# First LayerNorm fed feature first from the host, with its factor moved behind the matmuls, and a new order of loads and splits around the output projection of a pre-norm block

## The chip, the core and the metric

The kernel runs on one core of a Trainium2 chip, as one program in one launch. The metric is the device time of an execution in microseconds (us); lower is better. The kernel before was timed in three runs (median 1134.21 us, 1131.7 to 1136.86), and one more execution was profiled. TensorE (PE) does the matmuls, VectorE (DVE) and ScalarE (ACT) the elementwise work, GpSimd (POOL) a little of it, and SyncE (SP) issues all the DMAs shown here, in one queue: SP handles its instructions in order, and an instruction that has to wait holds up all behind it. The same is true of the other engines.

## The reference

One token sequence of 2048 tokens with 640 features passes through attention and a gated MLP, both behind a LayerNorm without parameters:

```python
def layernorm(x): return (x - mean(x)) / sqrt(var(x) + 1e-5)      # over the 640 features
qkv = layernorm(x) @ wqkv                    # 32 heads of 20 features
p   = softmax(where(0 <= i - j < 256, q @ k.T * 20**-0.5, -1e9))  # sliding window of 256
h   = x + (p @ v) @ wo
z   = gelu(layernorm(h) @ w_in)              # 1728 = 2 * 864 columns
g   = w_sp @ layernorm(z[:, 864:]) + b_sp    # 2048 x 2048 mixing of the tokens
out = h + (z[:, :864] * g) @ w_out
```

Everything is float32. The kernel keeps that accuracy with split products: an operand is written as a rounded part `hi` and a rest `lo`, and a product is hi\*hi + hi\*lo + lo\*hi, three matmuls.

## The kernel before

The 2048 tokens are 16 tiles of 128 (`NT`), the 640 features 5 blocks of 128 (`KD`). The order on PE, DVE, ACT and SP is the order in which the code is written (`manual_schedule`), so nothing overtakes anything on one engine; only POOL's order is left to a scheduler. The stages, with their place in the profiled execution:

- **V stage (0 to 92 us).** Per token tile i: `load_x` brings x token first (128 tokens x 640), `ln1` makes mean and variance (`bn_stats`, `bn_aggr`, + eps, and the power -1/2 on POOL, L74 to L77) and writes `xn = (x - mean) * rstd` in one DVE instruction (L80). `turn1` transposes the five blocks of xn on PE (L469, five matmuls with `ident`), and ACT and DVE take `hi` and `lo` out of PSUM into `xn_hi`, `xn_lo` (L473, L474), feature first. `vgemm` (L485 to L487) is two halves of 320 columns, 5 blocks, 3 products: 30 matmuls; ACT puts the result into `v_sb` (L488). The tiles 0 and 1 come while the weights `wv` are still being split (L560, L561). Also here: `wo` is loaded, split and stored to `wo_d` for later, and the first three pieces of `wqk` are loaded and split.
- **Q and K stage (92 to 245 us).** `qk_item(m, c)`: 128 of the 1280 q and k columns (m, 0 to 9) by 512 tokens (c, 0 to 3), 15 matmuls (L525 to L527). `split_qk` divides the result into three bf16 parts: ACT takes the first (L539), DVE the rest (L541), ACT the second (L543), POOL the third (L544); a DMA stores them in `qk_d`. From about 190 us on (`dense_tail`) each of the last twelve items is mixed, five steps an item, with `max_item`s of the attention: one score matmul and one DVE reduction each (L333, L339).
- **Attention (245 to 478 us).** 128 units s, each one block of 128 keys for four heads: row maxima, scores, exp on ACT, a mask on POOL, and p times v on PE (L425, `pv_item`), two units behind the scores. The last 15 units have no maxima left and wait for ACT. The sums of p come out as an extra row of v, row `DH` of `o_d`.
- **Output projection (473 to 562 us).** Per token tile: `norm_o` multiplies o by 1/sum (L162), `split_o` makes hi and lo (L168, L170, L171), `proj_o` is 30 matmuls (L100), `add_h` adds x (L1227) and stores h, `bn_h` and `scaled` make its LayerNorm, `turn_h` transposes it (L844) and stores it feature first in `hn_d`. In between lie the loads of o, of the sums (`rs`; for tokens from 512 on the reciprocals are formed once, `inv`, and go through `r_d`), of x again (`load_x2`), and `win1_prep`: w_in's first half, loaded in three steps into one buffer `wraw` (L780, L786) and turned into 16 tiles of split combinations (L715, L721, L136, L137). The first tiles' share of this runs inside the last attention units, as a generator `proj_early` that takes one step per unit from unit 97 on; the reciprocals of later tokens are further generators, `inverse_sums`.
- **MLP (562 to 1130 us).** `z_pair`, `z2_pair`, `first_gate`, `second_gate`: lists of steps that this change leaves as they are, but for three calls at the start of the list (`turn_h` of the last tile, and the opening of a pool).

## Time and profile before

| | |
|---|---|
| median of 3 runs | 1134.21 us (1131.7 to 1136.86) |
| the profiled execution | 1132.73 us; span 1130.9 us, so 1.8 us lie outside the span |
| granted TensorE clock, mean | 0.997 |
| PE busy | 1093.7 us, 97% of the span |
| DVE / ACT / POOL busy | 732.2 / 565.9 / 296.6 us |
| DMA | 171.78 MB |

In the rows that follow, a timeline row is: start in us, duration in us (of the whole group if it ends in xN), engine, line, operation, output<-input, shapes; in brackets how long the engine had been idle and who released it. Matmul durations overlap, so a matmul's cost is read from the starts of successive rows. A row of stretches gives, for each engine, busy us (and instructions), then the granted clock, the DMA engines' busy share and GB/s. A row of waits gives who waited for whom: us in total, times, longest.

### The profile page before, as it was taken

What the parts mean: (1) busy time and instruction counts of PE and PEld (TensorE: products, weight loads), DVE (VectorE), ACT (ScalarE), POOL (GpSimd) and SP (SyncE); (2) the same over time, 40 slices, a digit from 0 to 9 for tenths busy, and PEclk for the clock granted to TensorE, in tenths of its full rate; (3) what the DMA queues carried; (4) which work ended last, traced back from release to release, by engine and by line L of the source; (5) the groups of instructions that cost most, each with busy time, mean ns of one, the idle gap of its engine ahead of it and who ended that gap; (6) DMA issues with size and microseconds to landing.
All of it is one profiled execution on the core that took longest, in us unless ns stands there. A gap on an engine that the chain in (4) does not pass through costs nothing.

```text
span 1130.9 us, 28689 instructions
## 1 busy us (share of the span) xinstructions
PE 1093.7 (97%) x11180; PEld 986.3 (87%) x11180; DVE 732.2 (65%) x2060; ACT 565.9 (50%) x1169; POOL 296.6 (26%) x429
## 2 busy tenths in 40 slices
PE   8999999999999999889899999999999899999998
PEld 7998887667887777689799999999999799999998
DVE  6541123789999998478877678645458974656442
ACT  3433443249998989635566567433247521222210
POOL 3314444446666666612200011000001000000000
PEclk9999999999999999999999999999999999999999
DMA  5621346555565555489754522233251564444321
GB/s 183 224 72 68 136 141 239 176 178 170 184 188 175 181 170 158 143 241 305 255 185 165 181 90 76 85 122 101 100 162 57 176 193 135 123 148 138 103 87 61
DMA packets 83320, 171.78 MB, mean 152 GB/s; under 512 B 10944, under 2 KB 45248, under 8 KB 79296
## 3 DMA queue, kind: packets, MB, share of 16 engines
q1 hardware_dynamic: 83184, 169.95, 46.9%
q8 instruction: 88, 1.44, 0.6%
q14 instruction: 48, 0.39, 0.1%
HBM read 112.04 MB, written 57.87 MB: 150 GB/s over the span
## 4 chain that ended last, share of the span: by engine, by line
PE 74%; DVE 7%; DMA 7%; ACT 7%; issue 3%; POOL 1%; SPq 1%; DVEq 0%; ACTq 0%; POOLq 0%
PE g L1064 22%; PE out_ps L1129 8%; PE pv L425 5%; ACT pt L400 4%; PE zb L956 4%; PE qk L525 4%; PE qk L526 4%; PE qk L527 4%; PE bank L329 3%; PE bank L397 3%; PE zx L904 2%; PE zv L904 2%; DMA m<-o_d 2%; DMA wraw<-w_in_in 2%; PE zy L904 1%
## 5 line engine op out<-in xcount | busy, mean ns | idle before, releaser
L400 ACT ACTIVATE pt<-bank 128x384 f32<-128x384 f32 (+1 forms) x452 | 180.7, 477 | 19.9 <-PE bank L397 15.2
L721 ACT ACTIVATE aw<-fx 128x512 fp32r<-128x512 f32 (+2 forms) x160 | 93.5, 594 | 167.3 <-PE g L1064 122.6
L1064 PE MATMUL g<-zl,aw 128*128 128x432 f32 x768 | 171.8, 359 | 0.8 <-ACT zl L721 0.6
L339 DVE CUSTOM_DVE_ANT_0 junk<-bank,strip 128x288 bf16<-128x288 f32 x392 | 156.4, 454 | 14.0 <-PE bank L329 13.0
L1064 PEld LDWEIGHTS g<-zl,aw 128*128 128x128 f32 x768 | 143.7, 188 | 7.6 <-ACT zl L721 0.9
L425 PE MATMUL pv<-pt,v_sb 128*32 128x192 f32 (+3 forms) x1984 | 130.6, 322 | 7.5 <-ACT ot L441 3.5
L1064 PE MATMUL g<-ze,aw 128*128 128x432 f32 x576 | 134.8, 362 | 0.8 <-ACT aw L721 0.4
L715 DVE TENSOR_TENSOR aw<-fx,aw 128x512 fp32r<-128x512 f32 (+2 forms) x160 | 102.6, 646 | 37.9 <-ACT aw L721 36.7
L1064 PEld LDWEIGHTS g<-ze,aw 128*128 128x128 f32 x576 | 107.7, 189 | 7.0 <-ACT aw L721 1.6
L404 POOL TENSOR_SCALAR_AFFINE_SELECT pt<-pt 128x512 f32<-128x512 f32 x128 | 82.3, 644 | 61.9 <-ACT pt L400 58.2
L397 PE MATMUL bank<-slot 123*32 123x288 bf16 (+6 forms) x1296 | 94.0, 275 | 3.1 <-issue 2.2
L1129 PE MATMUL out_ps<-wout,y_sp 128*128 128x320 f32 (+1 forms) x630 | 96.2, 309 | 0.4 <-ACT y_sp L136 0.4
L956 PE MATMUL zb<-win,aw 128*128 128x432 f32 x480 | 95.3, 359 | 0.0
L1129 PEld LDWEIGHTS out_ps<-wout,y_sp 128*128 128x128 f32 (+1 forms) x630 | 94.1, 188 | 1.2 <-ACT y_sp L136 0.7
L329 PE MATMUL bank<-slot 120*32 120x288 bf16 (+6 forms) x1280 | 92.8, 277 | 1.9 <-DVE mcol L339 1.5
L956 PEld LDWEIGHTS zb<-win,aw 128*128 128x128 f32 x480 | 89.9, 187 | 5.0 <-ACT row L721 0.3
L86 POOL TENSOR_TENSOR mvz<-mvz,half 128x1 f32<-128x1 f32 x16 | 10.1, 633 | 303.3 <-DVE mvz L85 303.3
L541 DVE TENSOR_TENSOR rest<-qk,sg 128x512 f32<-128x512 f32 x40 | 27.7, 692 | 84.2 <-ACT sg L539 84.2
L425 PEld LDWEIGHTS pv<-pt,v_sb 128*32 128x32 f32 x1984 | 60.4, 110 | 18.7 <-issue 9.2
L715 DVE TENSOR_TENSOR row<-g,row 128x432 f32<-128x432 f32 x80 | 48.2, 604 | 37.6 <-PE g L1064 36.8
L407 POOL TENSOR_SCALAR_AFFINE_SELECT pt<-pt 128x512 f32<-128x512 f32 x112 | 72.5, 648 | 0.0
L397 PEld LDWEIGHTS <-slot 123*32 123x32 bf16 x1728 | 59.4, 97 | 14.1 <-issue 5.3
(185 smaller groups left out, 2233.0 us busy)
## 6 DMA issues: line engine op xcount, KB each, us to landing
slot<-qk_d SPq DMA_DIRECT2D x144, 160.0 KB
fx<-wsp_in SPq DMA_DIRECT2D x32, 512.0 KB
qk_d<-sg SPq DMA_DIRECT2D x40, 384.0 KB
fx<-hn_d SPq DMA_DIRECT2D x32, 320.0 KB
o_d<-ot SPq DMA_DIRECT2D x64, 128.0 KB
xb<-qk_d SPq DMA_DIRECT2D x48, 160.0 KB
z_d<-row SPq DMA_DIRECT2D x16, 432.0 KB
g_d<-row SPq DMA_DIRECT2D x16, 432.0 KB
```

What stands on the lines that cost most here:

```text
L329: nc.tensor.matmul(ps[32 * j:32 * j + 32, o:o + w], one(st, 120, 0, hh, q0, 32), k, start=True, stop=True, tile_position=(0, 32 * j))
L339: nc.vector.tensor_tensor_reduce(out=junk[:, :n], in0=ps[:, :n], in1=keep, scale=1.0, scalar=NEG, op0=OP.add, op1=OP.max, accum_out=m_cols ...
L397: nc.tensor.matmul(ps[32 * i:32 * i + 32, b + o:b + o + w], one(st, 123, 1, hh, k0, 32), q, start=True, stop=True, tile_position=(0, 32 * i))
L400: nc.scalar.activation(pt[:, hh, :n], ps[:, :n], AF.Exp, scale=SCALE)
L404: nc.gpsimd.affine_select(out=pt[:, :, :P], in_=pt[:, :, :P], pattern=[[0, 4], [1, P]], base=0, channel_multiplier=-1, compare_op=OP.is_ge ...
L407: nc.gpsimd.affine_select(out=pt[:, :, 256:], in_=pt[:, :, 256:], pattern=[[0, 4], [-1, P]], base=-1, channel_multiplier=1, compare_op=OP. ...
L425: nc.tensor.matmul(ps[32 * hh:32 * hh + 32, a - 512 * c:b - 512 * c], v_sb[:, kb, v0:v0 + 32], pt[:, hh, a - kb * P:b - kb * P], start=fir ...
L715: (eng or nc.vector).tensor_tensor(out=out, in0=a, in1=b, op=op)
L721: nc.scalar.activation(out, a, AF.Copy)
L956: nc.tensor.matmul(b[0][:, :HF], a[t][:, x, kk], win2[0][:, y, kk, h * HF:(h + 1) * HF], start=kk + x + y == 0, stop=kk == KD - 1 and x == 1)
L1064: nc.tensor.matmul(ps, w[m][:, x, k], zc[k][m][:, y], start=start and k + x + y == 0, stop=stop and k == 3 and x == 1, skip_group_check=True)
L1129: nc.tensor.matmul(ps[j][:, :HD], src[:w, a, k, :], e1["wout"][:w, b, k, j * HD:(j + 1) * HD], start=(k == 0 and a + b == 0), stop=(k == K ...
```

## The change

**First LayerNorm.** The host passes x a second time as `xt`, feature first per tile: xt[i] is 128 features x 5 blocks x 128 tokens. For tiles 4 to 15 nothing is transposed on PE any more: `load_xt` brings the tile, `load_mean` brings the means of its 128 tokens as a row on all partitions, and `turn1` subtracts it on DVE (L493), after which ACT and DVE make hi and lo from SBUF. x is still loaded token first for the statistics (`stats1`); its means and rstds go to DRAM, 4 bytes a partition (`store_mean`, `store_rstd`), since they must change from a column to a row. Tiles 0 to 3 keep the transposes, with `center1` in place of L80. The factor rstd is applied after the matmuls: for v as ACT's scale (`vgemm`), for q and k as a new DVE multiplication by a row of 512 rstds (`load_rstd`, 40 loads of 128 x 512), before the three-way split. wv's raw pieces share other buffers, and the order at the start is written anew.

**Output projection.** `proj_early` and `inverse_sums` are gone. A table `last_steps` says by unit what is issued: loads of o and sums from unit 117 on, x only from 119, w_in's first piece at 122 (its last at tile 1, into a buffer of its own), the reciprocals at 119, 122, 125 and 128, norm and split of tiles 0 to 3 between 121 and 128. The last three `pv_item`s stand behind `proj_o(0)`. In the loop over the tiles `norm_o` runs one tile further ahead and `bn_h` before the second half of the split; `turn_h(14)` moves behind step 0 of the list, `turn_h(15)` from behind step 2 to behind step 5.

The diff, cut to its core:

```diff
-            def ln1(i, between=None):
-                xn = tmp.tile([P, D], F32, tag="tb", bufs=2, name=f"xn{i}")
-                layernorm(xn, xts.pop(i), D, f"a{i}", between)
+            mvs, rows1, TURNED = {}, {}, 4
+            def load_xt(i):
+                t = tmp.tile([P, KD + 1, P], F32, tag="tb", bufs=3, name=f"xt_t{i}")
+                xns[i], rows1[i] = t[:, :KD], t[:, KD]
+                nc.sync.dma_start(xns[i], xt[i])
+            def stats1(i):
...
+            def center1(i):
...
+            def store_mean(i):
+                nc.sync.dma_start(mean_d[i].rearrange("(p a) -> p a", a=1), mvs[i][:, 0:1])
+            def store_rstd(i):
+                nc.sync.dma_start(rstd_d[i].rearrange("(p a) -> p a", a=1), mvs[i][:, 3:4])
+            def load_mean(i):
+                nc.sync.dma_start(rows1[i], every(mean_d[i], P))
             def turn1(i):
+                if i >= TURNED:
+                    hi, lo = (v[c][:, :, o * P:(o + 1) * P] for v in (xn_hi, xn_lo))
+                    nc.vector.tensor_tensor(out=xn, in0=xn, in1=rows1.pop(i)[:, None, :].to_broadcast([P, KD, P]),
+                                            op=OP.subtract)
+                    nc.scalar.activation(hi, xn, AF.Copy)
+                    nc.vector.tensor_tensor(out=lo, in0=xn, in1=hi.bitcast(F32), op=OP.subtract)
+                    return
...
             def split_qk(m, c, ps):
-                nc.scalar.activation(sg[:, 0, :], ps, AF.Copy)
+                rest = rests.pop(0)
+                nc.vector.tensor_tensor(out=rest, in0=ps, in1=rest, op=OP.mult)
                 yield
-                nc.vector.tensor_tensor(out=rest, in0=ps, in1=sg[:, 0, :], op=OP.subtract)
+                nc.scalar.activation(sg[:, 0, :], rest, AF.Copy)
                 yield
+                nc.vector.tensor_tensor(out=rest, in0=rest, in1=sg[:, 0, :], op=OP.subtract)
...
             for i in range(NT):
                 if i == 0:
                     vgemm(0)
-                    ln1(2, lambda: turn1(1))
+                    turn1(1)
+                    for n in (2, 3):
+                        stats1(n)
+                        center1(n)
+                        load_x(n + 3)
+                else:
+                    if i + 3 < NT:
+                        load_xt(i + 3)
+                        load_mean(i + 3)
+                    if i + 6 < NT:
+                        load_x(i + 6)
+                    if i + 1 < NT:
+                        turn1(i + 1)
+                if i + 4 < NT:
+                    stats1(i + 4)
+                    store_mean(i + 4)
+                store_rstd(i)
...
+    last_steps = {
+        117: lambda: (load_sums(0, False), load_o(0)),
+        118: lambda: (load_sums(1, False), load_o(1)),
...
+        122: lambda: (load_x2(4), load_win(0), first_sums(1)),
...
-                if hh == 2 + s - NU and s >= NU:
+                for u in {(NU, 1): [NU - 3], (NU + 1, 0): [NU - 2, NU - 1]}.get((s, hh), []):
+                    for _ in pv_item(u):
+                        pass
+                if (s, hh) in ((NU, 0), (NU + 1, 3)):
```

What this moves on the engines. On DVE, at the start of the program, the rows between the first tile's and the third tile's normalized x (xn1, xn2; `sta` and `mva` are statistics, `slot` the split weights wv, `bank` PSUM) were, before:

```order
L561 TENSOR_TENSOR slot0_1_99<-wvraw2_129,slot0_0_98 128x320
L561 TENSOR_TENSOR slot0_1_99<-wvraw4_131,slot0_0_98 128x320
L80 TENSOR_SCALAR xn1_195<-xt1_137,mva1_197 128x640
L74 BN_STATS sta2_244<-xt2_144 128x6 x2
L75 BN_AGGR mva2_245<-sta2_244 128x2
L76 TENSOR_SCALAR mva2_245<-mva2_245 128x1
L474 TENSOR_TENSOR xa_89<-bank3_118,xa_89 128x4x128
L474 TENSOR_TENSOR xa_89<-bank4_119,xa_89 128x128
L80 TENSOR_SCALAR xn2_243<-xt2_144,mva2_245 128x640
```

and in the changed kernel:

```order
L471 TENSOR_SCALAR xn1_206<-xt1_139,mva1_200 128x640
L606 TENSOR_TENSOR slot0_1_101<-wvraw2_131,slot0_0_100 128x320
L606 TENSOR_TENSOR slot0_1_101<-wvraw4_133,slot0_0_100 128x320
L506 TENSOR_TENSOR xa_91<-bank3_120,xa_91 128x4x128
L506 TENSOR_TENSOR xa_91<-bank4_121,xa_91 128x128
L464 BN_STATS sta2_256<-xt2_146 128x6 x2
L465 BN_AGGR mva2_257<-sta2_256 128x2
L466 TENSOR_SCALAR mva2_257<-mva2_257 128x1
L471 TENSOR_SCALAR xn2_263<-xt2_146,mva2_257 128x640
```

The two weight splits now stand behind xn1, and the statistics of tile 2 behind the lo part of tile 1 (the two rows into `xa`), which waits for tile 1's transposes.

On PE, at the same place, the first three value matmuls of tile 1 (`v`, L485 to L487 before, L517 to L519 now) and the transposes ahead of them were

```order
L469 MATMUL bank3_118<-ident_71,xn1_195 128x128 x4
L469 MATMUL bank4_119<-ident_71,xn1_195 128x128
L485 MATMUL v1_0_272<-slot0_0_98,xa_89 128x320
L486 MATMUL v1_0_272<-slot0_1_99,xa_89 128x320
L487 MATMUL v1_0_272<-slot0_0_98,xa_89 128x320
```

and are

```order
L501 MATMUL bank3_120<-ident_73,xn1_206 128x128 x4
L501 MATMUL bank4_121<-ident_73,xn1_206 128x128
L501 MATMUL bank5_122<-ident_73,xn2_263 128x128 x4
L501 MATMUL bank3_120<-ident_73,xn2_263 128x128
L517 MATMUL v1_0_312<-slot0_0_100,xa_91 128x320
L518 MATMUL v1_0_312<-slot0_1_101,xa_91 128x320
L519 MATMUL v1_0_312<-slot0_0_100,xa_91 128x320
```

Tile 2's transposes now stand ahead of tile 1's matmuls, so PE waits for xn2 before it may start them.

On SP, in the last attention units, the queue from the loads of x (`xh`) to the first store of inverse sums (`r_d`; `ot` are o's pieces on their way to `o_d`, `m` the buffer of o, `rs` the sums) was

```order
L141 DMA xh2_9422<-x_in 128x640
L141 DMA xh3_9423<-x_in 128x640
L141 DMA xh4_9424<-x_in 128x640
L444 DMA o_d_64<-ot7_0_0_9518 128x256
L152 DMA rs0_9416<-o_d_64 128x1x256
L157 DMA m1_9413<-o_d_64 32x5x256 x4
L444 DMA o_d_64<-ot7_0_1_9585 128x256
L152 DMA rs1_9417<-o_d_64 128x1x256
L157 DMA m1_9413<-o_d_64 32x5x256 x4
```

and is

```order
L440 DMA o_d_64<-ot7_0_0_9568 128x256
L440 DMA o_d_64<-ot7_0_1_9630 128x256
L154 DMA rs0_9466<-o_d_64 128x1x256
L161 DMA m1_9463<-o_d_64 32x5x256 x4
L154 DMA rs1_9467<-o_d_64 128x1x256
L161 DMA m1_9463<-o_d_64 32x5x256 x4
L146 DMA xh0_9470<-x_in 128x640
L146 DMA xh1_9471<-x_in 128x640
L440 DMA o_d_64<-ot7_1_0_9795 128x256
L440 DMA o_d_64<-ot7_1_1_9798 128x256
```

The loads of x moved behind the first sums and o; w_in's first piece, which came in tile 2 of the projection, now comes right after x.

More of the change, by code (lines that the diff above doesn't have):

```diff
@@ L551, in block_kernel @@
             load_x(0)
-            wv_raw = [tmp.tile([P, D], F32, tag="wraw", bufs=5, name=f"wvraw{k}") for k in range(KD)]
+            wv_raw = [tmp.tile([P, D], F32, tag=("wraw", "wqh")[k > 2], bufs=(3, 4)[k > 2], name=f"wvraw{k}")
+                      for k in range(KD)]
             for j, c in enumerate(halves):
@@ L785, in win1_prep @@
                 yield
-        nc.sync.dma_start(raw[:, 0], src[4 * P:])
-        yield
-        yield
-        for j in range(2):
-            split(*two(last[j]), raw[:, 0, j])
-        yield
     def win2_prep(raw):
@@ L1269, in block_kernel @@
             turn_h(i - 2)
[L1270 to L1271 removed]
     for _ in w1:
[L1273 removed]
+        raise ValueError("w_in")
     w2p = None
```

249 lines of the change are left out of this document (127 added, 122 removed).

## The prediction

> **What bounds the kernel now.** I read the page first, then the stretches (busy time by engine), then PE's waits and the timelines of the two stages that change. The page:
>
> ```profile
> span 1130.9 us, 28689 instructions
> PE 1093.7 (97%) x11180; PEld 986.3 (87%) x11180; DVE 732.2 (65%) x2060; ACT 565.9 (50%) x1169; POOL 296.6 (26%) x429
> ```
>
> PE is the bound, and all that it is not busy is 1130.9 - 1093.7 = 37.2 us. So the change can gain in two ways only: by taking work off PE, or by closing these gaps. PE's waits from the last attention units to the first steps of the MLP:
>
> ```profile
> PE ht_ps L844 <- ACT hn L91: 5.5, 5, 2.8
> PE zx L904 <- ACT ho L721: 2.7, 1, 2.7
> PE pv L425 <- DVE ot L443: 1.4, 1, 1.4
> PE pv L425 <- POOL pt L404: 0.7, 1, 0.7
> PE pv L425 <- POOL pt L407: 0.5, 1, 0.5
> ```
>
> That is 10.8 us in one stage, the largest place of idle PE in the span. The stretch of that stage (PE, PEld, DVE, ACT, POOL, clock, DMA share, GB/s), and the chain that ended last, at its DMAs:
>
> ```profile
> 485.00:560.00 75.00, 69.15 (x479) 67.10 (x478) 63.74 (x130) 38.02 (x59) 20.49 (x30) 1.00 0.85 270
> ...
> 454.31 5.53 DMA o_d<-ot
> ...
> 492.18 6.62 DMA wraw<-w_in_in
> ```
>
> DVE is busy 85% and the DMA engines 85%: PE is not held up by one engine's throughput but by single pieces that come late. 5.53 us for a store of 128 KB behind five loads of x, 6.62 us for the load of w_in that ACT and DVE wait for.
>
> **V stage: transposes removed.** The steady pace with transposes, and a tile without:
>
> ```profile
> 37.98 0.71 PE L469 MATMUL bank<-ident,xn 128*128 128x128 f32 x5
> ...
> 42.93 0.71 PE L469 MATMUL bank<-ident,xn 128*128 128x128 f32 x5
> ...
> 85.26 0.31 PE L485 MATMUL bank<-slot,xb 128*128 128x320 f32 x1
> ...
> 89.66 0.31 PE L485 MATMUL bank<-slot,xb 128*128 128x320 f32 x1
> ...
> 91.86 0.39 PE L525 MATMUL qk<-xa,wqh 128*128 128x512 f32 x1
> ```
>
> A tile with its five transposes takes 42.93 - 37.98 = 4.95 us; the last tiles have 30 matmuls and no transposes between them and take 89.66 - 85.26 = 4.40. Twelve tiles lose their transposes: 12 x 0.55 = **6.6 us** gained, if the new feed keeps this pace.
>
> DVE's share of it is one subtraction and one lo part from SBUF per tile, in place of the normalization and a lo part from PSUM. The nearest rows, same size, one with the same broadcast operand (L162):
>
> ```profile
> L171 DVE TENSOR_TENSOR xb<-m,xb 128x640 fp32r<-128x640 f32 x13 | 10.6, 817 | 1.5 <-ACT xb L170 1.5
> L162 DVE TENSOR_TENSOR m<-m,rs 128x640 f32<-128x640 f32 x12 | 9.8, 817 | 4.4 <-DMA m<-o_d 3.3 <-issue 1.2
> ```
>
> So 1.63 us for the two. With the statistics, read from the rows of tile 3 below (0.88 + 0.21 + 0.15 = 1.24), DVE has 2.9 us of work in 4.40: hidden, with 1.5 us of cover a tile. ACT does as much as before. The extra DMA (x a second time, 320 KB a tile) is issued three tiles ahead; I put it at nothing here and price its failure under the rivals.
>
> **The start is worse.** DVE and PE rows between tile 1 and tile 2:
>
> ```profile
> 13.46 0.89 DVE L561 TENSOR_TENSOR slot<-wvraw,slot 128x320 fp32r<-128x320 f32 x2
> 14.40 0.61 DVE L80 TENSOR_SCALAR xn<-xt,mva 128x640 f32<-128x640 f32 x1
> ...
> 16.55 0.89 DVE L474 TENSOR_TENSOR xa<-bank,xa 128x512 fp32r<-128x512 f32 x2 [0.31 <-ACT xa L473]
> ...
> 17.88 0.88 DVE L74 BATCH_NORM_STATS2 sta<-xt 128x6 f32<-128x320 f32 x2
> 18.79 0.21 DVE L75 BATCH_NORM_AGGREGATE mva<-sta 128x2 f32<-128x12 f32 x1
> 19.03 0.15 DVE L76 TENSOR_SCALAR mva<-mva 128x1 f32<-128x1 f32 x1
> ...
> 16.57 0.41 PE L485 MATMUL v<-slot,xa 128*128 128x320 f32 x1 [0.58 <-ACT xa L473]
> ...
> 23.60 0.39 PE L485 MATMUL v<-slot,xa 128*128 128x320 f32 x1
> ```
>
> Tile 1's normalization (0.61) now stands ahead of the two weight splits (13.46), for which PE's first tile waits, so all behind it is 0.6 later: tile 1's lo part ends at 17.44 + 0.6 = 18.0. Only then come tile 2's statistics (1.24) and its subtraction (0.61): 19.9. PE now has tile 2's transposes ahead of tile 1's matmuls, so these begin at 19.9 + 0.7 = 20.6, not 16.57. Then 4.40, the transposes of tile 3 (0.55) and tile 2's matmuls at 25.5, against 23.60: **1.9 us** lost of the 6.6. Bounds: 0 (if PE catches up through shorter waits later; before, it waits there too) and 4.0 (20.6 - 16.57).
>
> PE stands still from the end of tile 1's transposes (16.57 - 0.58 + 0.6 = 16.6) to 19.9: 3.3 us. What such a gap does to the clock, from the stretches around PE's gap at 896 us:
>
> ```profile
> 896.00:898.00 2.00, 0.12 (x1) 0.00 (x0) 2.00 (x4) 1.06 (x3) 0.00 (x0) 1.00 0.46 118
> 898.00:900.00 2.00, 1.70 (x6) 1.63 (x7) 2.00 (x5) 1.17 (x2) 0.00 (x0) 0.52 0.88 293
> ```
>
> After 1.9 us without work the granted clock was 0.52 for the next 2 us. If that happens here, about 3 us at half speed cost 1.5; the wait of 2.8 us in the list above cost no clock (1.00 over its whole stretch), so it need not. I take the middle, **0.7**. The Trainium skill ("TensorE: Matmul & The Clock Gate", What's actually happening) has the gate act on a free-running window of about 3.4 us without activity, then at half speed. By that rule the price here is 0 or 1.7, by the phase of the window; the trace agrees on the half, and at 896 us a shorter gap was enough.
>
> **Q and K stage: one more DVE instruction an item.** In the first 28 items DVE has no reductions beside it and PE sets the pace: nothing. In the last twelve, DVE's rows over one item:
>
> ```profile
> 234.32 0.69 DVE L541 TENSOR_TENSOR rest<-qk,sg 128x512 f32<-128x512 f32 x1
> 234.93 0.55 DVE L339 CUSTOM_DVE_ANT_0 junk<-bank,mask 128x384 bf16<-128x384 f32 x1
> 235.51 0.56 DVE L339 CUSTOM_DVE_ANT_0 junk<-bank,mask 128x384 bf16<-128x384 f32 x1
> 236.40 0.56 DVE L339 CUSTOM_DVE_ANT_0 junk<-bank,mask 128x384 bf16<-128x384 f32 x1 [0.31 <-PE bank L333]
> ...
> 238.72 0.69 DVE L541 TENSOR_TENSOR rest<-qk,sg 128x512 f32<-128x512 f32 x1
> ```
>
> The period is 238.72 - 234.32 = 4.40, set by PE. Back to back DVE needs 0.61 for L541 (234.93 - 234.32) and 0.58 for a reduction (235.51 - 234.93). Five reductions and two such instructions are 2.90 + 1.22 = 4.12, still under 4.40, but the second waits for ACT's first part (up to 0.3 more): 4.1 to 4.4. I take **0.3 us** in all, at the end of the stage, where DVE is behind; the bounds are 0 and, if each item took 4.7, 12 x 0.3 = 3.6. Behind the waiting DVE instruction stand the reductions that free PE's three banks; PE feels it after two of them. The 40 loads of rstd rows (256 KB each) are issued one item ahead, behind a store that waits for the same POOL instruction as their buffer, so they add no wait on SP.
>
> **Output projection: the gaps.** PE's own pace there, from the transposes:
>
> ```profile
> 487.43 0.75 PE L844 MATMUL ht_ps<-ident,hn 128*128 128x128 f32 x5
> ...
> 516.46 0.71 PE L844 MATMUL ht_ps<-ident,hn 128*128 128x128 f32 x5
> ...
> 536.25 0.71 PE L844 MATMUL ht_ps<-ident,hn 128*128 128x128 f32 x5
> ...
> 557.77 0.71 PE L844 MATMUL ht_ps<-ident,hn 128*128 128x128 f32 x5
> 559.84 0.77 PE L844 MATMUL ht_ps<-ident,hn 128*128 128x128 f32 x5 [1.37 <-ACT hn L91]
> ```
>
> Four undisturbed tiles: (536.25 - 516.46) / 4 = 4.95. Thirteen tiles from 487.43 to 557.77 would be 64.35 at that pace and are 70.34: 6.0 lost. With 1.4 before tile 14's transposes, 2.7 at zx and 2.6 at the three pv waits, 12.7 us are to be had. What the change does to each:
>
> - The pv waits: `proj_o(0)` fills the wait for POOL; and DVE no longer sits with a late reciprocal (the store of 5.53 no longer stands behind x) when it should copy `ot`.
> - Inside the loop: w_in's first and last piece come several tiles earlier than they are used, norm and split of tiles 0 to 3 lie in units where DVE is idle, o comes a tile or more ahead. That leaves DVE less to do in the 75 us than the 63.74 of the row, and PE's own 14 x 4.95 = 69.3 stays the longest.
> - Tile 14's wait and zx: the transposes now have a step between them and their LayerNorm, and w_in's last split no longer stands ahead of zx's operands on ACT.
>
> What is late next: DVE at 90% will now and then be behind (tile 3 has six instructions for w_in, tile 4 a reciprocal), and the DMA engines stay nearly as busy. I leave a fifth: **10.2 us** gained; bounds 12.7 and, if the waits only change their names, 4 (the pv and the zx part alone are harder to lose).
>
> **Sum.** -6.6 + 1.9 + 0.7 + 0.3 - 10.2 = -13.9. The profiled execution took 1132.73: 1118.8. The median lies 1134.21 - 1132.73 = 1.5 above it: **1120.3 us**.
>
> **Rivals.**
> 1. *The projection stays bound by late pieces.* For it: DVE and DMA at 85%, with the same bytes but for 1.3 MB moved ahead; against: four tiles in a row ran undisturbed amid that traffic. Half the gain goes, +5 to +6: 1126.
> 2. *All gaps close* and PE keeps its clock: -6.6 + 1.9 - 12.7 = -17.4: 1116.8.
> 3. *Slower: the mean's round trip paces the V stage.* SP, in one tile, waits for the statistics, stores the mean, and one tile later holds everything until that store has landed, because the load of the row reads it. A tile then costs the landing plus the issue of three DMAs. The rows:
>
> ```profile
> 380.67 1.91 DMA o_d<-ot
> ...
> 20.00:90.00 70.00, 69.13 (x490) 68.83 (x489) 33.99 (x89) 27.72 (x64) 18.63 (x20) 1.00 0.40 139
> ...
> 37.16 0.38 SPq L456 DMA_DIRECT2D xt<-x_in  x1
> ```
>
> At 1.91 + 3 x 0.38 = 3.1 it hides behind 4.40; it decides from a landing of 3.3 on. At the 5.53 above, reached behind 1.6 MB of loads, a tile takes 6.7: 12 x 2.3 less a lead of some 5 us: +22, so 1142. For it: this stage's DMA grows by half (139 GB/s over 70 us are 9.7 MB; 12 x 0.39 MB of xt and means come on top). Against: its engines were busy 40%.
> The Trainium skill ("DMA: Bandwidth & Descriptors", Specifications) gives 512 B as the least for full rate and says that below it a DMA reads, modifies and writes; the stores of means are 4 B a partition. [...] No run here shows a store of that form.
> 4. *No visible change*: the start and the last items cost their bounds (4.0 + 1.5 + 3.6) and the projection gives 4: 1133.
>
> **Chances.** Forecast 0.60, rival 1 0.18, rival 2 0.08, rival 3 0.06, rival 4 0.08. A difference of 0.5% (5.7 us) is what a measurement here can tell. Faster by more: 0.60 + 0.08 and most of rival 1, 0.82; within: 0.12; slower: 0.06. Range: from just under rival 2 to just over the slow end of rival 1, 1115.5 to 1128.5, which leaves out rivals 3 and 4 and a little more.
>
> **What would show it.** The first Q and K matmul at about 87.7 instead of 91.86; V tiles 4.40 apart; PE's gap near 17 to 20 us, with or without a clock under 1. The item period near 235 us still 4.40. The projection's transposes 4.95 apart from first to last, no wait for `hn` over 1 us, zx without a wait. Wrong if the V tiles are 5 us or more apart, if SP waits for means longer than 3 us, or if the projection still shows gaps of 5 us in all.

## The result and the profile after

The changed kernel takes 1207.3 us (median of 6 runs, 1204.0 to 1210.3); the kernel before, beside it, 1132.95 (6 runs, 1129.7 to 1136.9). The ratio is 1.066, 95% interval 1.064 to 1.068: 74 us slower, where 14 us faster was forecast. The page after, to be set against the two lines of before:

```profile
span 1206.7 us, 28771 instructions
PE 1118.3 (93%) x11120; PEld 1002.5 (83%) x11120; DVE 762.4 (63%) x2089; ACT 566.5 (47%) x1157; POOL 298.5 (25%) x429
```

PE has 60 instructions fewer and yet is busy 24.6 us longer, a first sign of a lower clock; its idle time grew from 37.2 to 88.4 us. PE's timelines, cut at the first matmul of each stage, say where the 75.8 us of the two profiled executions lie:

| stage, by its first PE instruction | before | after | difference |
|---|---|---|---|
| start to first Q/K matmul (V) | 91.86 | 160.14 | +68.3 |
| to first pv matmul (Q, K, first reductions) | 157.5 | 162.9 | +5.5 |
| to first projection matmul (attention) | 224.2 | 221.6 | -2.5 |
| to first zx matmul (output projection) | 91.0 | 92.8 | +1.8 |
| to the end | 566.4 | 569.2 | +2.8 |

The -2.5 is bookkeeping: the first projection now stands ahead of the last pv items. The V stage in stretches (PE, PEld, DVE, ACT, POOL, clock, DMA share, GB/s), first of after, then of before:

```profile
20.00:60.00 40.00, 30.98 (x172) 29.29 (x171) 13.52 (x34) 8.14 (x15) 6.09 (x8) 0.84 0.67 101
60.00:100.00 40.00, 22.35 (x104) 20.27 (x102) 9.44 (x20) 8.72 (x16) 6.71 (x7) 0.80 0.98 142
100.00:140.00 40.00, 24.72 (x101) 22.50 (x102) 9.16 (x19) 5.33 (x11) 1.64 (x3) 0.71 0.72 84
```

```profile
20.00:60.00 40.00, 39.13 (x279) 38.85 (x278) 22.54 (x60) 16.61 (x38) 12.09 (x13) 1.00 0.59 202
60.00:100.00 40.00, 40.00 (x260) 38.41 (x259) 12.46 (x32) 15.32 (x34) 11.64 (x10) 1.00 0.12 43
```

No compute engine is the bound after: PE has work for 22 to 31 of 40 us, at a granted clock of 0.71 to 0.84. The DMA engines look like it from 60 to 100 us, oddly: packets stood on them for 0.98 of the time, and moved 142 GB/s, where before 0.59 moved 202. What SP and PE wait for, from 20 to 160 us (total, times, longest):

```profile
SPq L486 <- DMA mean_d<-mva: 89.2, 12, 8.4
PE v L517 <- ACT xb L495: 32.1, 7, 6.5
```

And the loop itself, first SP's issues, then the chain that ended last:

```profile
127.12 0.32 SPq L486 DMA_DIRECT2D xt_t<-mean_d  x1
127.53 0.38 SPq L477 DMA_DIRECT2D mean_d<-mva  x1
...
136.58 0.33 SPq L486 DMA_DIRECT2D xt_t<-mean_d  x1
```

```profile
118.10 8.96 DMA mean_d<-mva
127.53 9.03 DMA mean_d<-mva
```

SP issues the store of a tile's means at 127.53; the next instruction that needs it, the load of the row, can go at 136.58, and only behind that does SP store the next tile's means. This tile costs 136.58 - 127.12 = 9.5 us, 9.0 of them the landing, for which rival 3 had taken 5.53. Over the twelve tiles the landings took 7.5 to 10.8 us.

### The profile page after: what moved, and what is told of

Its sections match the earlier page's. It is cut to its first block, busy times and chain, and to the rows that moved or that the text cites. A ratio compares the mean times of both kernels' runs of the same rounds, so it can differ in the third digit from the quotient of the medians.

```text
span 1206.7 us, 28771 instructions
## 1 busy us (share of the span) xinstructions
PE 1118.3 (93%) x11120; PEld 1002.5 (83%) x11120; DVE 762.4 (63%) x2089; ACT 566.5 (47%) x1157; POOL 298.5 (25%) x429
## 4 chain that ended last, share of the span: by engine, by line
PE 65%; DMA 10%; ACT 7%; DVE 4%; issue 2%; POOL 1%; SPq 1%; DVEq 0%; ACTq 0%; POOLq 0%
PE g L1116 20%; PE out_ps L1181 8%; PE zb L1008 6%; ACT pt L396 5%; PE pv L421 4%; PE qk L568 3%; PE qk L569 3%; PE qk L570 3%; PE bank L340 3%; PE bank L393 3%; PE wo_ps L102 2%; DMA mean_d<-mva 2%; PE zx L956 2%; PE zv L956 2%; DMA rest<-rstd_d 1%
## 5 line engine op out<-in xcount | busy, mean ns | idle before, releaser
L350 DVE CUSTOM_DVE_ANT_0 junk<-bank,strip 128x288 bf16<-128x288 f32 x392 | 155.9, 453 | 13.7 <-PE bank L340 13.4
L340 PE MATMUL bank<-slot 120*32 120x288 bf16 (+7 forms) x1280 | 94.8, 277 | 3.4 <-issue 1.4
L393 PE MATMUL bank<-slot 123*32 123x288 bf16 (+7 forms) x1296 | 95.1, 275 | 0.9 <-issue 0.9
L421 PEld LDWEIGHTS pv<-pt,v_sb 128*32 128x32 f32 x1984 | 61.8, 110 | 20.3 <-issue 12.2
L777 DVE TENSOR_TENSOR row<-g,row 128x432 f32<-128x432 f32 x80 | 48.2, 603 | 37.2 <-PE g L1116 36.7
L588 POOL TENSOR_TENSOR sg<-rest,sg 128x512 bf16<-128x512 f32 x40 | 46.7, 1167 | 88.5 <-ACT sg L587 57.4
```

The costliest lines, as they stand in the source:

```text
L340: nc.tensor.matmul(ps[32 * j:32 * j + 32, o:o + w], one(st, 120, 0, hh, q0, 32), k, start=True, stop=True, tile_position=(0, 32 * j))
L350: nc.vector.tensor_tensor_reduce(out=junk[:, :n], in0=ps[:, :n], in1=keep, scale=1.0, scalar=NEG, op0=OP.add, op1=OP.max, accum_out=m_cols ...
L393: nc.tensor.matmul(ps[32 * i:32 * i + 32, b + o:b + o + w], one(st, 123, 1, hh, k0, 32), q, start=True, stop=True, tile_position=(0, 32 * i))
L421: nc.tensor.matmul(ps[32 * hh:32 * hh + 32, a - 512 * c:b - 512 * c], v_sb[:, kb, v0:v0 + 32], pt[:, hh, a - kb * P:b - kb * P], start=fir ...
L777: (eng or nc.vector).tensor_tensor(out=out, in0=a, in1=b, op=op)
```

## The experiments

Two theories stood after the comparison. **Round trip**: SP waits for each store, and that alone sets the pace. **Occupancy**: the 28 stores of 128 pieces of 4 B hold up the DMA engines, whoever waits. Apart from V, there was the projection, whose 10.2 us had not come.

### The two halves apart

`e1_head` has the change's first half (V, Q, K) with the old projection, `e2_tail` the reverse; there is no other edit.

> The change's first half alone: x feature first, LayerNorm's factor behind the matmuls, the mean through DRAM; the output projection as before. Theory (the mean's round trip paces the V stage and the loss is all there): the shift of 71 us that the changed kernel's trace has at the first projection matmul (544.70 against 473.46) comes whole, and the old projection adds nothing: 1133 + 71 = 1204 us, first Q/K matmul near 160. Rival (the projection's new order gained its 10 us after all and the V stage lost more): 1207 + 10 = 1217 us.

Measured: 1210.4 us, ratio 1.069 (1.063 to 1.075). The first Q/K matmul came at 167.74, later than the theory's 160, with the same V stage as the changed kernel; why, the runs don't show.

> The change's second half alone: the new order of loads and splits at the output projection, with V, Q and K as before. Theory (VectorE stands 7.8 us behind the reciprocal of sums 512 to 1023, whose load queues behind residual tiles and spatial weights, and TensorE then waits 3.9 + 2.7 us and runs at half clock): the tail loses as it does in the changed kernel, 118.7 us from the first projection matmul to the tenth z group against 113.2 before, so 1133 + 5 = 1138 us. Rival (the prediction's: the new order closes 10.2 us of gaps, and lost them in the changed kernel only because the first half had shifted its transfers): 1123 us.

Measured: 1136.4 us, ratio 1.0023 (0.9998 to 1.0048). The whole loss is the first half's; the second half is worth nothing by itself, 0 to 5 us on the wrong side.

### No wait, another form, fewer stores

`e3_no_wait`:

```
-                nc.sync.dma_start(rows1[i], every(mean_d[i], P))
+                nc.sync.dma_start(rows1[i], every(xt[i, 0, 0], P))
```

> The changed kernel with the row of means read from an input tensor in place of the stored means, so that no load waits for a store; all 28 stores of 128 x 4 B stay. What it leaves out: the true means of tiles 4 to 15. Theory (SP's queue waits for each store's landing, about 9 us, and that alone sets the tile period): V tiles 4.4 to 5 us apart, first Q/K matmul at 88 to 95, 1207 - 68 = about 1139 us. Rival (the 4-byte stores occupy the DMA engines, which stood at 0.9 to 1.0 of their time at only 100 GB/s, and transfers come late whoever waits): tiles still 7 us or more apart, above 1165 us.

Measured: 1194.0 us, ratio 1.053 (1.046 to 1.060); first Q/K matmul at 144.68. With the wait gone, only 15 of the 68 us went. The DMA engines from 20 to 90 us show the rival's picture, and SP's waits something else:

```profile
q1 hardware_dynamic: 6517, 8.63, 98.8%
```

```profile
SPq L540 <- DMA mean_d<-mva: 14.3, 3, 5.6
SPq L480 <- DMA mean_d<-mva: 12.3, 4, 5.8
SPq L477 <- DMA mean_d<-mva: 10.4, 2, 5.9
```

SP still waits for stores of means, ahead of instructions that don't read them. The program's order of SP's instructions tells why: every DMA takes the next of eight semaphores, and so waits until the DMA issued eight before it has landed. A tile at this place has just eight:

```
L486 DMA xt_t_459<-xt_in 128x128 [waits DMAHW0_49]
L450 DMA xt_462<-x_in 128x640 [waits DMAHW1_49]
L477 DMA mean_d<-mva_468 128x1 [waits DMAHW2_49,DVE_49]
L480 DMA rstd_d<-mva_279 128x1 [waits DMAHW3_49,Pool_49]
L540 DMA woraw_476<-wo_in 128x640 [waits DMAHW4_49,Pool_49]
L552 DMA wo_d<-woh_422 128x640 [waits DMAHW5_49]
L552 DMA wo_d<-wol_423 128x640 [waits DMAHW6_49]
L457 DMA xt_t_517<-xt_in 128x640 [waits DMAHW7_49,Activation_49]
...
L477 DMA mean_d<-mva_526 128x1 [waits DMAHW2_49,DVE_49]
```

So here a tile's store of means waits for that of the tile before: the experiment took the wait that I saw and left one that I had not seen. It tells the two theories apart less well than I had meant.

`e4_row_store` turns the means to one row by a matmul and stores 512 B from one partition, behind the products of the tile (lines left out are marked):

```
...
+                nc.tensor.matmul(row, mvs[i][:, 0:1].to_broadcast([P, P]), ident, start=True, stop=True)
...
+                nc.vector.tensor_copy(out=sb, in_=row[r])
+                nc.sync.dma_start(mean_d[i:i + 1, :], sb)
```

> The changed kernel with each tile's means stored as one row of 512 B from one partition (a matmul turns the column, VectorE copies the row) in place of 128 pieces of 4 B; the load still waits for the store, and the stores of the other statistic stay as columns. Theory A (the 4-byte form is what lands late): landing 2 to 4 us, tiles 4.5 to 6 us apart, 1140 to 1160 us. Theory B (any store followed by a dependent load costs this on a queue with large transfers in front): landing still 7 to 9 us, 1195 to 1210 us.

Measured: 1205.8 us, ratio 1.063 (1.056 to 1.070). SP's wait for this one piece was still up to 9.1 us (67.2 in 12). That looks like theory B, but each tile's other column store was still queued beside it; `e9_row_only` below takes that away.

`e5_pe_mean` makes the row by that matmul and lets DVE read it from PSUM; `e7_pe_mean_stores` puts the mean's store back, unread; `e6_no_rstd_store` is the changed kernel without the other statistic's stores.

> The changed kernel with the row of means made by one matmul (the mean column repeated over 128 columns, against the identity) and read by VectorE from PSUM: no store and no load of means; the 16 column stores of the other statistic stay. The run without the wait (1194 us, DMA engines 98.8% busy at 124 GB/s from 20 to 90 us) leaves two causes for the engines' time. Theory S (the 4-byte pieces of the stores, about 0.35 us of an engine each): one store of 128 pieces a tile is left, 2.8 us of 16 engines, beside 4.8 us of large transfers: tiles 6 to 7.5 us apart at first, 1150 to 1165 us. Theory L (the load that reads one 512 B row 128 times, about 0.55 us of an engine for each reading, and 0.13 us for each 4-byte piece): tiles 4.5 to 5.8 us apart, 1133 to 1143 us.

Measured: 1164.2 us, ratio 1.028 (1.024 to 1.033); first Q/K matmul at 118.75: theory S's number. One look inside, at the DMA engines from 98 to 104 us, while a tile of x (issued at 98.49) comes in behind a column store (issued at 95.50; three more are issued from 102.34 on), and then in the kernel before, a tile of x and three of weights from 62 to 68 us (packets, MB, share of 16 engines):

```profile
q1 hardware_dynamic: 228, 0.38, 63.6%
```

```profile
q1 hardware_dynamic: 575, 1.31, 61.8%
```

A packet took 0.636 x 6 x 16 / 228 = 0.27 us on average, the stores' own among them, against 0.10. By size, the packets of 2560 B took 0.57 us on average against 0.12, and those of 4 B 0.01 in both. So transfers beside such a store are slow themselves, whoever waits.

> The kernel with the means' row from a matmul, and the column store of the means put back although nobody reads it: both stores a tile, no load of the row, no wait. Theory S: as without the wait, 1185 to 1195 us. Theory L: 1137 to 1150 us.

Measured: 1183.5 us, ratio 1.045 (1.041 to 1.050); first Q/K matmul at 132.96. One more store a tile, which nobody reads or waits for, costs 19 us. (SP's eight in flight are at work here too: it waits 24 us for stores of means.)

> The changed kernel without the 16 column stores of the other statistic (its rows are read from an input, so Q and K are scaled by other numbers); the means' store, wait and load stay. Theory S: half of the 4-byte pieces gone, tiles 6 to 7.5 us apart, 1155 to 1170 us. Theory L: the load of the means' row still takes 4.4 us of all engines a tile and the store's landing still stands ahead of it: tiles 8 us or more apart, 1185 to 1200 us.

Measured: 1212.0 us, ratio 1.071 (1.066 to 1.075). That is above both ranges: S had half of the loss go, and it did not. SP's wait and the chain:

```profile
SPq L486 <- DMA mean_d<-mva: 97.8, 12, 9.0
```

```profile
130.80 8.98 DMA mean_d<-mva
```

With one column store a tile and a wait for it, the landing of 9 us is the whole pace, and the second store hides behind it. Both theories hold, then, and feed on the same thing: a column store lands late, and that is paid through the load that reads it (`e6`), or through the eighth DMA behind it and the slow packets beside it (`e3`, `e5`, `e7`). Undoing one of these shows little while another stands. How the loss without the named wait divides between the eight in flight and the slow packets, these runs don't separate.

`e8_pe_rows` makes both rows by matmuls and normalizes x in full, so that nothing goes through DRAM:

```
...
+                    for j, op in ((0, OP.subtract), (3, OP.mult)):
+                        row = ps[:, j * P:j * P + P]
+                        nc.tensor.matmul(row, mvs[i][:, j:j + 1].to_broadcast([P, P]), ident, start=True, stop=True)
+                        nc.vector.tensor_tensor(out=xn, in0=xn, in1=row[:, None, :].to_broadcast([P, KD, P]), op=op)
```

> The changed kernel with both rows from matmuls, x normalized in full before the products, V, Q and K as in the kernel before: no small store, no row through DRAM, x feature first kept, and the new projection order. Both theories: tiles about 4.6 us apart (15 products' 4.40 and two small matmuls), first Q/K matmul near 89; with the projection's order worth nothing (1.0023 by itself) 1131 to 1136 us. VectorE has one more pass a tile, 0.82 us, for which a period of 4.6 leaves room.

Measured: 1153.7 us, ratio 1.020 (1.016 to 1.023). Both theories missed, by the experiment's own fault:

```profile
32.94 0.38 PE L496 MATMUL bank<-ident,mva 128*128 128x128 f32 x2
34.33 0.46 PE L496 MATMUL bank<-ident,mva 128*128 128x128 f32 x2 [1.01 <-DVE xt_t L497]
39.02 0.38 PE L496 MATMUL bank<-ident,mva 128*128 128x128 f32 x2
```

The second row goes to the bank from which DVE reads the first, so PE waits 1.01 us a tile. Tiles come 6.08 us apart: the products' 4.40 and this wait leave 0.67 for two matmuls of this kind, more than the 0.55 of the five transposes that they replace.

### What in the store costs

`e9_row_only` is the row store without the other statistic's stores; `e10_loads_only` has no small store at all, only the load of a row.

> The changed kernel with the means stored as one 512 B row per tile, waited for and loaded as before, and no column store left in the loop (the other statistic's 16 stores are left out and its rows read from an input, so Q and K are scaled by other numbers). Theory F (a store of 128 pieces of 4 B is what makes a round trip long, its own and every transfer's beside it): landing 3 to 4.5 us, tiles 5 to 6.5 us apart, first Q/K matmul at 100 to 115, 1142 to 1158 us. Theory R (any load that waits for a store in one queue costs this, whatever the form): landing 8 to 9 us, first Q/K matmul past 150, 1195 to 1212 us.

Measured: 1152.8 us, ratio 1.017 (1.012 to 1.021); first Q/K matmul at 98.71. The chain:

```profile
57.05 3.14 DMA mean_d<-mrow
60.20 3.63 DMA xt_t<-mean_d
```

One piece of 512 B landed in 3.1 us, so theory R falls: it is the form. Against `e10` below, the round trip with the matmul that makes the row (0.67 / 2 us a tile by `e8`) still costs 98.71 - 87.95 = 10.8 us in V.

> The changed kernel with the load of the means' row alone (128 readings of one 512 B row, here of an input) and no small store of either kind in the loop. What it leaves out: the true means and scales. Theory F: the loads cost little, tiles 4.4 to 5 us apart, first Q/K matmul at 92 to 100, 1133 to 1145 us. Theory L (the repeated reading holds the engines): first Q/K matmul past 110, above 1150 us.

Measured: 1135.4 us, ratio 1.0017 (0.9993 to 1.0041). V ends here:

```profile
87.95 0.39 PE L568 MATMUL qk<-xa,wqh 128*128 128x512 f32 x1
```

The prediction had 87.7 for this instruction. `e11_before_columns` goes the other way: the kernel before, with one store a tile of a constant that nobody reads.

```
+                nc.sync.dma_start(c_d[i].rearrange("(p a) -> p a", a=1), half)
```

> The kernel before with 16 column stores added, one a tile of the V stage, 128 pieces of 4 B of a constant into a tensor that nobody reads: no wait is added anywhere. Theory F (about 3 us of all 16 DMA engines a store, 44 us over 14 stores by the run with one store a tile): the V stage's own transfers, which take 0.59 of the engines from 20 to 60 us, come late and the first Q/K matmul moves from 91.9 to 100 to 115: 1141 to 1156 us. Rival (a store that nobody waits for is hidden, since x is loaded three tiles ahead): 1131 to 1136 us.

Measured: 1143.4 us, ratio 1.0082 (1.0054 to 1.0110), though nobody reads what is stored. The stretches and the first Q/K matmul:

```profile
20.00:60.00 40.00, 35.61 (x244) 34.45 (x243) 20.86 (x45) 14.95 (x34) 11.21 (x11) 0.98 1.03 161
60.00:100.00 40.00, 37.84 (x259) 37.38 (x259) 16.75 (x44) 13.04 (x30) 8.01 (x9) 0.98 0.76 99
```

```profile
100.22 0.39 PE L526 MATMUL qk<-xa,wqh 128*128 128x512 f32 x1
```

Against before, the engines are busy (1.03 - 0.59 + 0.76 - 0.12) x 40 us x 16 = 691 engine-us more, for 8 KB of data: 43 us a store, or 2.7 us of all sixteen, as the profile counts a packet's time (overlapping packets add up, hence 1.03). This time is not in the store's own packets. By size, from 20 to 100 us, all packets of 4 B took 37 engine-us, against 4 before. Those of 2 KB and more, the other transfers', took 1145 against 450, with the same median of 0.10 us but up to 6.6 us, against 1.3, for one. SP, with its eight in flight, stood 29 us for these stores.

Then the same pieces 64 B apart (`e13_pieces_apart`, its edit here against `e11`), and pieces of 512 B that lie side by side (`e14_512B_pieces`):

```
-    c_d = dram.tile([NT, P], F32, name="c_d")
+    c_d = dram.tile([NT, P, 16], F32, name="c_d")
...
-                nc.sync.dma_start(c_d[i].rearrange("(p a) -> p a", a=1), half)
+                nc.sync.dma_start(c_d[i][:, 0:1], half)
```

> The kernel before with 16 column stores of a constant as in the run that cost 10.4 us, but each 4 B piece 64 B from the next, so that no two share a 64 B stretch of the tensor. Theory P (128 tiny pieces cost about 2.6 us of all engines whatever their place): first Q/K matmul at 98 to 102, 1140 to 1146 us. Theory N (neighbouring pieces of one stretch wait for each other): first Q/K matmul at 92 to 94, 1131 to 1137 us.

Measured: 1134.3 us, ratio 1.0002 (0.9982 to 1.0022):

```profile
20.00:60.00 40.00, 39.13 (x278) 38.85 (x278) 22.55 (x60) 16.60 (x38) 12.09 (x13) 1.00 0.62 201
60.00:100.00 40.00, 40.00 (x261) 38.40 (x260) 12.46 (x32) 15.31 (x34) 11.63 (x10) 1.00 0.15 44
```

```profile
91.81 0.39 PE L526 MATMUL qk<-xa,wqh 128*128 128x512 f32 x1
```

> The kernel before with 16 added stores of 128 pieces of 512 B (64 KB each, 128 times the bytes of the column stores), waited for by nobody. Theory P, with the size deciding: 64 KB at the 47 engine-us per MB of this stage's large transfers is 3 engine-us, 0.2 us of 16 engines, against 41 engine-us for 512 B in 4 B pieces: first Q/K matmul at 92 to 94, 1131 to 1137 us. Rival (a small store costs by its 128 pieces, whatever they hold): 1140 us or more.

Measured: 1133.3 us, ratio 1.0002 (0.9981 to 1.0022). Theory N holds: as many pieces, as small, cost (0.03 + 0.03) x 640 / 16 = 2.4 engine-us a store when none has a neighbour (`e13`), about an eighteenth. The landing follows: from issue to the last update of its semaphore a store took 12.2 us in `e11` (median of 16), 3.2 in `e13` and 3.1 in `e14`. Neither count nor size nor neighbours alone set the price: the pieces of 512 B lie side by side too, and the ratio stays at 1.0002. Of the forms run here, only pieces that are both small and adjacent are dear. In the changed kernel itself, all 28 stores kept and only moved apart:

> The changed kernel with all 28 stores of 128 x 4 B kept, but each piece 64 B from the next; the rows that are loaded come from an input, as in the run without the wait (1194 us). What it leaves out: the true means and scales in V, Q and K. Theory N (only neighbouring pieces hold the engines): as with the loads alone, first Q/K matmul at 88 to 92, 1134 to 1141 us. Rival (the stores of a statistic that VectorE or GpSimd has just written, beside the loads of one row, cost more than a constant's): first Q/K matmul past 105, above 1150 us.

Measured: 1133.6 us, ratio 1.0014 (0.9991 to 1.0036), against 1194.0 for `e3`, which has the pieces adjacent and differs otherwise only in loading the factor's rows from what was stored:

```profile
88.33 0.39 PE L568 MATMUL qk<-xa,wqh 128*128 128x512 f32 x1
```

### The projection's order

The second half by itself keeps PE waiting as long as before. One wait of DVE's, and PE's, of `e2_tail`, in the stretch for which the prediction had listed 10.8 us:

```profile
DVE inv L206 <- DMA inv<-o_d: 7.0, 1, 7.0
...
PE ht_ps L826 <- ACT hn L91: 4.7, 3, 4.0
PE wo_ps L100 <- DVE xb L178: 2.5, 1, 2.5
PE zx L886 <- ACT row L713: 1.8, 1, 1.8
PE pv L419 <- POOL pt L398: 1.0, 2, 0.6
PE pv L419 <- DVE ot L437: 0.4, 1, 0.4
```

10.4 us, under other names. `e12_tail_order` takes the splits of tiles 1 and 2 ahead of the reciprocal for which DVE stands 7.0 us:

```
-        125: lambda: inverse_recip(1),
-        126: lambda: (inverse_store(1), inverse_load(2), ready(1)),
-        127: lambda: (load_o(2), ready(2), norm_o(3)),
+        125: lambda: ready(1),
+        126: lambda: (inverse_load(2), load_o(2), ready(2), norm_o(3)),
+        127: lambda: (inverse_recip(1), inverse_store(1)),
...
-        129: lambda: (load_o(3), norm_o(4)),
+        129: lambda: load_o(3),
```

with tile 4's scaling behind the first residual sum.

> The change's second half alone (1.0023 of before) with VectorE's order mended: the splits of tiles 1 and 2 and the scaling of tile 3 before the reciprocal of sums 512 to 1023, which waits for its load until 476.8, and the scaling of tile 4 behind the first residual sum. Theory (VectorE's 7 us behind that load are what eats the new order's gain): TensorE's waits of 2.5 and 4.0 us at tiles 1 and 0, and 2.8 us at half clock behind the second, go: 1136 - 8 = 1128 us. Rival (the next transfer, the sums' way through DRAM, is as late and the waits only move): 1134 to 1137 us.

Measured: 1138.0 us, ratio 1.0028 (1.0010 to 1.0047). The rival's picture, 1 us above its range: tile 1's wait of 2.5 went, and tile 0's transposes waited longer. ACT and PE there:

```profile
491.45 0.56 ACT L713 ACTIVATE zl<-wraw 128x432 fp32r<-128x432 f32 x1 [13.40 <-DVE wraw L707]
491.92 0.91 ACT L91 ACTIVATE hn<-xh,mvc 128x640 f32<-128x640 f32 x1
...
492.88 1.33 PE L826 MATMUL ht_ps<-ident,hn 128*128 128x128 f32 x5 [7.01 <-ACT hn L91]
```

Tile 0's statistics were ready at 485, but DVE then waited 3.5 us for tile 4's row of sums, a split of w_in stood behind that, ACT waited 13.4 us for the split, and `hn(0)` stood behind ACT. `e15_tail_order2` moves tile 4's scaling behind tile 1's residual sum.

> The second half alone with VectorE's order mended further: tile 4 is scaled behind the residual sum of tile 1, tile 5 one step later, so that nothing ahead of the first two tiles' statistics waits for the sums' way through DRAM. Theory (in-order VectorE and ScalarE carried that wait to the first transpose row, which stood 7.0 us in the run before and 4.0 us in the half as written): the first row comes at about 487 in place of 493, and the steady 4.95 from there: 1136 - 6 to 8 = 1128 to 1130 us. Rival (tile 4's product at PE then waits instead, 4 to 7 us later on): 1133 to 1138 us.

Measured: 1133.6 us, ratio 0.9996 (0.9977 to 1.0014). The first transposes did come at 487.38; PE's waits are now 7.2 us for `hn` in six pieces, none over 2.7. That is the rival's time again, but not its mechanism: PE waits for tile 4's product nowhere that long (1.1 us for a residual sum is the longest wait at the products).

### A version that beats both

`e16_pe_transposes` is the first half without DRAM: a transpose of the repeated column gives the same row on every partition, both before DVE reads, and the start's order nearer to before.

```
...
+                    for j in (0, 3):
+                        nc.tensor.transpose(ps[:, j * P:j * P + P], mvs[i][:, j:j + 1].to_broadcast([P, P]), ident)
+                    for j, op in ((0, OP.subtract), (3, OP.mult)):
+                        row = ps[:, j * P:j * P + P]
+                        nc.vector.tensor_tensor(out=xn, in0=xn, in1=row[:, None, :].to_broadcast([P, KD, P]), op=op)
```

> The change's first half with both rows from TensorE transposes of the repeated statistic columns (two of 0.11 us a tile in place of five), both issued before VectorE reads either, x normalized in full so that Q and K are as in the kernel before, the start's order near that of before, the old projection order. Theory: tiles 4.40 + 0.22 = 4.62 us apart in place of 4.95, 12 tiles: first Q/K matmul at 88 to 90, 1129 to 1131 us against 1133. Rival (VectorE's pass more and the start eat it): 1132 to 1136 us.

Measured: 1129.1 us, ratio 0.9959 (0.9941 to 0.9977):

```profile
27.46 0.38 PE L503 MATMUL bank<-ident,mva 128*128 128x128 f32 x2
32.08 0.38 PE L503 MATMUL bank<-ident,mva 128*128 128x128 f32 x2
...
87.26 0.39 PE L578 MATMUL qk<-xa,wqh 128*128 128x512 f32 x1
```

4.62 us a tile, as worked out, and the stage 4.6 us shorter.

> Both rows from two transposes (0.9959 of before by itself) and the projection's new order with VectorE's order mended twice (0.9996 by itself), in full. Theory (the two halves add): 0.9955 of before, 1127 to 1130 us. Rival (the projection's transfers meet others once V ends 4.6 us earlier, or gain their 10 us there): outside 1125 to 1132 us.

Measured: 1125.4 us, ratio 0.9941 (0.9921 to 0.9962), the fastest here, and 1.6 us under the theory's range. Whether the projection's order adds anything to `e16` stays open: the intervals overlap.

## Why the prediction was wrong

**The step that failed** is the sentence on the extra DMA: "I put it at nothing here". It counted the bytes of x and of the rows and passed over 28 stores whose bytes are nothing. Rival 3 named the place and one of the two mechanisms, but gave it 0.06 and 22 us; against the V stage without stores (`e10`) it cost 160.14 - 87.95 = 72. Its mechanism, SP waiting for the landing, was not all: with that wait gone 144.68 - 87.95 = 57 us stayed (`e3`), through the eighth DMA and the slow packets. Two things were mis-sized:

- *The landing.* I took 5.53 us, a store of before that stood behind five loads; measured 9.0. No store of before had that form, so no row of before was a bound. The Trainium skill ("DMA: Bandwidth & Descriptors", Anatomy of one DMA) gives about 2.0 us as the fixed cost of a DMA on the GpSimd path. These DMAs are issued by SP, so it is no figure for them; here the row in `e9` landed in 3.1 us, the columns in 9.0.
- *The engines.* "Its engines were busy 40%" stood against the rival. It said nothing of how long a packet stands: one column store a tile made 0.59 into 1.03 in `e11`, with 161 GB/s moved in place of 202, and the added time lay in the other transfers' packets. The Trainium skill (same page, Specifications) has a DMA below 512 B read, modify and write. Pieces of 4 B were dear here only side by side; apart they were as good as free (`e13`), so here the size alone did not decide.

The clock came on top: with waits of up to 6.5 us between tiles PE was granted 0.71 to 0.84, and was busy 24.6 us longer with fewer matmuls.

**V: transposes, start, clock, -6.6 + 1.9 + 0.7.** Right, once the stores are out of the way: 87.95 in `e10` against 91.86 is -3.9; the terms make -4.0. In `e10` tile 2's matmuls begin at 26.27, 2.7 later than before (1.9 + 0.7 forecast), and the tiles then come 39.55 - 35.15 = 4.40 apart:

```profile
19.26 0.77 PE L501 MATMUL bank<-ident,xn 128*128 128x128 f32 x5 [3.18 <-DVE xn L471]
...
26.27 0.39 PE L517 MATMUL v<-slot,xa 128*128 128x320 f32 x1
...
35.15 0.31 PE L517 MATMUL v<-slot,xa 128*128 128x320 f32 x1
...
39.55 0.31 PE L517 MATMUL v<-slot,xa 128*128 128x320 f32 x1
```

The split at the start was off. The gap was 3.18 us (3.3 forecast), and tile 1's matmuls began at 19.79 in place of 20.6. But they took 26.27 - 19.79 = 6.5 us to tile 2's in place of 4.95, at a granted clock of 0.53 from 20 to 22 us and 0.62 from 22 to 24: 1.5 us of clock, the upper bound, where 0.7 was taken. The two errors, 0.8 each, cancel by luck.

**Q and K, +0.3 with a bound of 3.6.** Wrong: +5.5, and the waits point elsewhere than at DVE's instruction count. That the loads "add no wait on SP" is nearly true (SP stood 4.8 us at them in the stage); but a load that is issued in time can land late:

```profile
237.85 0.37 SPq L561 DMA_DIRECT2D rest<-rstd_d  x1
...
244.35 0.69 DVE L582 TENSOR_TENSOR rest<-qk,rest 128x512 f32<-128x512 f32 x1 [5.23 <-DMA rest<-rstd_d]
```

```profile
PE qk L568 <- DVE rest L582: 4.0, 4, 2.0
```

The row of factors, issued at 237.85 among the loads of the score stacks, came over 6 us later; DVE waited 13.5 us for such rows in all, and PE 4.0 for DVE. `e10`, whose V stage is undisturbed, has 162.8 us in this stage; `e16`, without these rows and without the multiplication, 156.9. No run has the multiplication without its row, so what the instruction itself costs stays open.

**Projection, -10.2.** Wrong. Half of the premise held: the steady pace of 4.95 came (574.58, 579.52 in the list below), and w_in and the residual tiles were early. What failed is "DVE no longer sits with a late reciprocal", and "I leave a fifth":

```profile
552.11 0.95 DVE L208 RECIPROCAL inv<-inv 128x128 f32<-128x128 f32 x1 [7.82 <-DMA inv<-o_d]
...
554.74 0.87 PE L102 MATMUL wo_ps<-xb,xb 128*128 128x320 f32 x2 [3.94 <-DVE xb L180]
...
568.02 1.07 PE L896 MATMUL ht_ps<-ident,hn 128*128 128x128 f32 x5 [2.73 <-ACT hn L93]
574.58 0.71 PE L896 MATMUL ht_ps<-ident,hn 128*128 128x128 f32 x5
579.52 0.71 PE L896 MATMUL ht_ps<-ident,hn 128*128 128x128 f32 x5
```

The sums go store, load, reciprocal, store, load; the new order put one of these steps on DVE ahead of splits that need none of them. Mending that moved the wait to the next step behind the same path, and then to ACT. PE's waits added up to 10.8 before, 10.4 in the new order (`e2`) and some 12 in `e15`: the lower bound of 4 us, "if the waits only change their names", should have been 0. So the forecast would have failed without the stores too: `e10`, with no small store, takes 1135.4 us, 15 above it. That is about what Q and K (5.2 more than forecast) and the projection (10.2 less gained) make together.

## What to carry to other kernels

Do not write one value a partition into a dense row in DRAM: here such a store landed in 9 us, slowed what moved beside it, and, with eight DMAs in flight at most, held up SP even where nobody read it. Letting a TensorE transpose of the repeated column make the row on all partitions cost 0.11 us each here. Storing one row still cost 10.8 us in V where a load waited for it, and pieces 64 B apart cost nothing to store; reading them back as a row was not run. Before pricing a DMA by the rows of a profile, ask whether any row has its form; if none has, the dearest row is no upper bound. And a wait that ends on a path of several DMAs is not removed by reordering the engines in front of it: it moves to the next instruction in order.

## What the runs showed of the hardware that was not expected

That a store of neighbouring 4 B pieces lands late and makes the packets of other transfers stand, and one of pieces 64 B apart does neither. What in the memory does it is not shown; only spacings of 4 and 64 B were run. How a landing looks, in the changed kernel, in 40 slices from 117 to 128 us (busy tenths of the DMA engines):

```profile
DMA  6652446507992669995531100000000000000000
```

The mean's store, issued at 118.10, landed at 127.06; the last packet ended at 123.5, while the 16 updates of the store's semaphore came one by one from 122.1 to 127.1. The last 3.6 us of the landing are thus not engine time, and a DMA queue that looks idle can still keep its waiter.

Left open: the last 2.8 us of the stage table (this part took from 565.8 to 571.9 us in the profiled executions), and the attention stage, which took from 219.6 to 227.2 us in the profiled executions without a pattern that these runs explain. Both are readings of single executions; the verdicts above rest on medians.
